# A linear-attention and gated-MLP mixer on one core: operands of the spatial products laid at equal residues, sums in place, a fixed order at the stage border

## The chip, the core and the metric

The kernel runs on one core of one Trainium2 chip. The core has five engines that run their own queues in order: TensorE (PE; its weight loads are listed as PEld), VectorE (DVE), ScalarE (ACT), GpSimd (POOL) and SyncE (SP, which here only issues transfers). They meet through semaphores. Data lie in SBUF (128 partitions) and PE writes to PSUM (8 banks of 512 floats per partition). A matmul has a stationary operand (at most 128 x 128, loaded first) and a moving one (128 x up to 512 columns). The metric is device time in microseconds (us) of one execution; the median of several runs is compared.

## The reference

All numbers are float32. After a layernorm of x, the outputs of two mixers are added to x:

```python
xn = _layernorm(x)                       # x: 1 x 2048 x 512
# A: linear attention, 32 heads of 16, phi = softmax(+) and softmax(-) of a per-head projection
num = einsum(phi_q, phi_k^T v);  den = einsum(phi_q, sum phi_k) + 1e-6;  A = (num / den) @ wo
# B: gated MLP with a spatial product over the 2048 tokens
z = gelu(xn @ w_in)                      # 2048 x 1376, halves z1 and z2 of 688 columns
z2 = layernorm(z2)
g = einsum("ts,bsf->btf", w_sp, z2) + b_sp[None, :, None]   # 2048 x 2048 times 2048 x 688
B = (z1 * g) @ w_out
return x + A + B
```

## The kernel before

Every product is computed from operands split into two parts, h (rounded to float32r) and l (what is left over). `mm3` (line 55) issues three matmuls for one product: h by h, h by l and l by h, lines 57, 58 and 59 in the profile. `round_h` (line 47) makes h, on ACT at line 49, and `rest_l` (line 52) makes l on DVE, line 53; `b_parts` (line 592) is the pair of them. The l part reads the h part, so DVE waits for ACT each time.

There are four stages. The first projects q, k, v and z1 and gathers the attention's sums. The second (loop at line 738) projects z2 from the weight tile w2 with `zproj` (line 138): 16 rows s of 128 tokens, each 2 halves of 344 columns (FC), tile zps in PSUM. ACT applies gelu and the normalisation (`normed`, line 730), and after every second s `b_split` (line 707) makes the moving operands of the spatial stage from the pair n = s // 2. The third is the spatial stage. The fourth projects the gated rows and the attention's output and adds them up.

**The spatial stage** computes w_sp @ z2 with the seven products of a Strassen-Winograd scheme on 2 x 2 blocks. NC = 32 steps n, each one (i, q) of `SEQ`: i counts 8 pairs of output rows of 128 tokens, q 4 chunks of the contracted tokens (for the last i in the order 1, 2, 3, 0). In a step, `products` (line 790) issues for each of the seven products P1, P2, P6, P5, P7, P3, P4, in this order (`FORM`), two chunks k of three matmuls: 42 matmuls of 344 columns, into seven PSUM banks of g that accumulate over the four steps of an i. The stationary operands (A11, A12, A22, S1 to S4) come from w_sp, the moving ones (B11, B21, B22, T1 to T4) from z2. P1 is A11 by B11, P2 A12 by B21, P6 S2 by T2, P5 S1 by T1, P7 S3 by T3, P3 S4 by B22, P4 A22 by T4.

`load_a` (line 597) loads the raw weights of a step (tiles wf) through SP's queue, in two transfers of 256 KB, into tiles f0 and f1 with two buffers each. `prep_a` (line 606) makes the A operands of a step: four sums on DVE (lines 621 to 625) into a tile S of its own, and four roundings and remainders. The tile that holds a pair of them has all h parts, then all l parts, each part [names][2][128] floats. Steps of even n take them from the right pool ws, those of odd n from the left pool hl1, which lies where w2 was. `b_tile` (line 694) hands out tiles of 1408 floats (SL) for B operands, seen as [a][b][352]: a is h or l, b one of two operands. B11 of the pairs 2q and 2q+1 share a tile; B22 and B21, T1 and T3, T2 and T4 have one for each pair. `b_split` takes three differences per pair into T (lines 710, 714, 719), on DVE. Line 739 gives `zproj` the halves in reversed order for odd s, so that the four quarters of z lie in the order 0, 1, 3, 2.

The loop at line 887 has, for a step n: at the second step of an i the load of z1 on POOL's queue (`load_z1`), `products`, at the fourth step `drain` (line 801: one copy on ACT, seven combinations of the PSUM banks on DVE into the tile c), then `load_a(n + 3)` and `prep_a(n + 2)`, then `gate` (line 816: gelu on ACT, the product with c on DVE) and its `turn`, which transposes on DVE and stores u in eight transfers on SP (lines 837 and 839; on POOL for i = 6). Three steps from the end the preparation of the fourth stage begins (`stage_w`, `first_gate`).

Otherwise the order of the instructions on each engine is that of a scheduler which works on the program's order and its own estimate of time; `tc.issue_after` pins single instructions. At the border of the second and third stage the last pairs of B and the first steps of A are made by DVE and ACT at once, while PE works on the last zps and the first g.

SBUF is laid out by pools stacked from the left (cst, xz, w1 ...) and from the right (pad, ws, zw, w2 ...). A tile's first byte follows from the sizes of all tiles ahead of it; the tiles named pad and gap hold nothing and only shift what comes after.

Of the kernel before, what the change touches and what calls it, by code (L numbers as in the profile page):

```python
# [18 lines left out]
P = 128  # L19
# [22 lines left out]
def mixer(ctx: ExitStack, tc: tile.TileContext, x, x_t, wv, wqkT, phi_bd, wo, w_in, wst, b_r, w_out, out):  # L42
# [50 lines left out]
    cst.tile([P, 8], F32, name="pad")  # L93
# [44 lines left out]
    def zproj(ps, s, w, order=(0, 1), wide=False):  # L138
# [15 lines left out]
        for k, j in enumerate(order):  # L154
            for c in range(ND):
                cs = slice(c * P, (c + 1) * P)
                zproj.last = mm3(p[k][:, :FC], (t[:, 0, cs], t[:, 1, cs]), (w[j][0][:, c], w[j][1][:, c]), c == 0, c == ND - 1)
# [386 lines left out]
    mid.enter_context(right("pad", 1)).tile([P, P + 8], F32, name="pad")  # L544
# [5 lines left out]
    w2_pool.tile([P, QP // 2], F32, name="gap")  # L550
# [41 lines left out]
    def b_parts(h, l, src):  # L592
        rounded = round_h(act, h, src)
        rest_l(l, src, h)
        return rounded

    def load_a(n):
        i, q = SEQ[n]
        f = []
        for k in range(2):  # L600
            t = ws.tile([P, QC, P], F32, tag=f"f{k}", bufs=2, name="wf")
            sp.dma_start(t, wst[2 * i + k, :, q * QC:(q + 1) * QC, :])
            f.append(t.rearrange("p (k two) t -> p two k t", two=2))
        return f

    def prep_a(n, f):
# [4 lines left out]

        def parts(names, src):
            t = pl.tile([P, 2, len(names), 2, P], F32R, tag="".join(names), name="A")
            prep_a.last = b_parts(t[:, 0], t[:, 1], src)
            for k, m in enumerate(names):
                ops[m] = t[:, 0, k], t[:, 1, k]

        sums = (sm[0].tile([P, 4, 2, P], F32, name="S") if sm else
                zw.tile([P, 4, FC], F32, tag=("T", "z2")[n], bufs=n + 1, name="S").rearrange("p a b -> p (a b)")[:, :8 * P].rearrange("p (a k b) -> p a k b", a=4, k=2))
        parts(("A11", "A12"), a)  # L620
        dve.tensor_tensor(sums[:, 0], b[:, 0], b[:, 1], op=ALU.add)
# [8 lines left out]
    hl, raw, A, sm = [ws, None], {}, {}, []  # L630
    NE = 2
    with ExitStack() as p1:
# [40 lines left out]
        A[0] = prep_a(0, raw.pop(0))  # L673
        sp.dma_start(kvT_d, kvT)
# [30 lines left out]
    B, b11 = [], None  # L705

    def b_split(z, n):
        nonlocal b11
        tt = zw.tile([P, 4, FC], F32, tag="T", name="T")
        dve.tensor_tensor(tt[:, 0:2], z[:, 1:3], z[:, 0:2], op=ALU.subtract)  # L710
        if n % 2 == 0:
            b11 = b_tile()
        b_parts(b11[:, 0, n % 2], b11[:, 1, n % 2], z[:, 0])
        dve.tensor_tensor(tt[:, 2], z[:, 2], tt[:, 0], op=ALU.subtract)
        ops = {"B11": (b11[:, 0, n % 2], b11[:, 1, n % 2])}
# [3 lines left out]
        dve.tensor_tensor(tt[:, 3], z[:, 3], tt[:, 2], op=ALU.subtract)  # L719
        t = b_tile()  # L720
        b_parts(t[:, 0], t[:, 1], tt[:, 0:2])
        ops["T1"], ops["T3"] = [(t[:, 0, k], t[:, 1, k]) for k in range(2)]
        t = b_tile()
        b_parts(t[:, 0], t[:, 1], tt[:, 2:4])
        ops["T2"], ops["T4"] = [(t[:, 0, k], t[:, 1, k]) for k in range(2)]
# [12 lines left out]
    for s in range(NT):  # L738
# [21 lines left out]
        if s == NT - 1:  # L760
            for k in range(2):
                normed(*late.pop(0), ins)
# [384 lines left out]
```

## Time and profile before

| what | value |
|---|---|
| runs of the kernel before | 612.50, 614.14, 614.09 us; median 614.09 |
| the profiled execution's own time | 613.86 us |
| its span (first to last instruction) | 612.1 us |
| granted TensorE clock | 1.000 |
| PE busy | 605.6 us (99%) |
| DVE busy | 520.0 us (85%) |
| ACT busy | 259.5 us (42%) |
| POOL busy | 132.4 us (22%) |
| spatial stage, first to last start of a matmul | 275.7 to 487.3 us |

Lines of a group read: source line, engine, operation, output <- inputs with shapes, count, then busy time, mean duration in ns and the engine's idle time ahead of them. For a tile they read: count, shortest/median/longest duration in ns, and the starts of the first and the last in us. Lines of the timeline read: start in us, duration in us, engine, line, operation, and in brackets how long the engine had been idle and what released it. A matmul's duration covers its way through the array, so consecutive ones overlap, and the pace of PE is the distance between starts. Lines with a window A:B give its length, then the busy time of each engine with its count of instructions, the clock, the share of the DMA engines and GB/s.

### The profile page before, as it was taken

How to read it: one execution, taken by the hardware profiler on the slowest of the kernel's cores; microseconds unless marked ns; L12 is line 12 of the kernel's file. 1: busy time of each engine (PE TensorE's matmuls, PEld its weight loads, DVE VectorE, ACT ScalarE, POOL GpSimd, SP SyncE). 2: the span in 40 equal slices, each digit the busy share in tenths (PEclk: the TensorE clock that was granted, in tenths of full speed). 3: DMA queues.
4: the chain of work that ended last, by engine and by line, in shares of the span. 5: the costliest groups of instructions: out<-in, count | busy, mean ns of one | idle time of the engine just before them, and what ended most of it. 6: DMA issues, size and time to landing. Idle time of an engine off the chain costs nothing.

```text
span 612.1 us, 11394 instructions
## 1 busy us (share of the span) xinstructions
PE 605.6 (99%) x4286; PEld 551.1 (90%) x4286; DVE 520.0 (85%) x930; ACT 259.5 (42%) x414; POOL 132.4 (22%) x231
## 2 busy tenths in 40 slices
PE   8999999999999999999999999999999999999997
PEld 6888888888888999999999999999999988777776
DVE  5999999999988578899888896877879999999932
ACT  4653324423433547887534433342335443332220
POOL 4122232333111014552000001000200041143430
PEclk9999999999999999999999999999999999999999
DMA  8557877566537848001455636555556899799792
GB/s 320 187 131 176 217 176 188 149 163 169 139 107 213 261 177 308 2 1 35 142 124 153 180 98 178 135 163 153 166 161 185 254 295 292 184 285 276 181 254 69
DMA packets 57950, 107.85 MB, mean 176 GB/s; under 512 B 12392, under 2 KB 24552, under 8 KB 57672
## 3 DMA queue, kind: packets, MB, share of 16 engines
q1 hardware_dynamic: 43656, 65.22, 35.3%
q0 software_dynamic: 11936, 36.28, 23.9%
q10 hardware_dynamic: 2304, 5.64, 2.4%
q8 instruction: 33, 0.54, 0.4%
q14 instruction: 21, 0.17, 0.1%
HBM read 66.85 MB, written 35.54 MB: 167 GB/s over the span
## 4 chain that ended last, share of the span: by engine, by line
PE 82%; DVE 8%; DMA 5%; issue 2%; ACT 1%; SPq 0%; POOL 0%; ACTq 0%; DVEq 0%; POOLq 0%
PE proj L58 7%; PE proj L57 7%; PE proj L59 7%; PE g L57 7%; PE g L58 7%; PE g L59 7%; PE zps L57 6%; PE zps L59 6%; PE zps L58 6%; PE pout L57 5%; PE pout L59 5%; PE pout L58 5%; DMA wf<-in_wst 3%; DVE A L53 2%; DMA z1t<-z_d 1%
## 5 line engine op out<-in xcount | busy, mean ns | idle before, releaser
L57 PE MATMUL g<-B,A 128*128 128x344 f32 x448 | 142.8, 320 | 0.6 <-DVE c L810 0.4
L58 PE MATMUL g<-B,A 128*128 128x344 f32 x448 | 142.3, 319 | 0.0
L59 PE MATMUL g<-B,A 128*128 128x344 f32 x448 | 138.9, 318 | 0.0
L57 PEld LDWEIGHTS g<-B,A 128*128 128x128 f32 x448 | 84.0, 188 | 1.6 <-DVE c L810 0.7
L58 PEld LDWEIGHTS g<-B,A 128*128 128x128 f32 x448 | 84.0, 188 | 0.0
L59 PEld LDWEIGHTS g<-B,A 128*128 128x128 f32 x448 | 83.6, 188 | 0.0
L49 ACT ACTIVATE A<-S 128x512 fp32r<-128x512 f32 x64 | 39.3, 628 | 74.8 <-DVE S L622 63.8
L57 PE MATMUL proj<-wqk_h,xT 128*128 128x512 f32 x128 | 50.1, 391 | 0.0
L59 PE MATMUL proj<-wqk_h,xT 128*128 128x512 f32 x128 | 49.8, 389 | 0.0
L58 PE MATMUL proj<-wqk_l,xT 128*128 128x512 f32 x128 | 49.8, 389 | 0.0
L125 ACT ACTIVATE e<-e,r_x 128x1024 f32<-128x1024 f32 x26 | 29.8, 1149 | 42.3 <-DVE e L124 41.3
L53 DVE TENSOR_TENSOR A<-S,A 128x512 fp32r<-128x512 f32 x64 | 42.8, 684 | 2.9 <-ACT A L49 2.8
L49 ACT ACTIVATE A<-wf 128x512 fp32r<-128x512 f32 (+1 forms) x64 | 32.7, 515 | 24.6 <-DMA wf<-in_wst 18.8
L57 PE MATMUL zps<-w1h,xT 128*128 128x344 f32 (+2 forms) x128 | 40.8, 320 | 0.0
L58 PE MATMUL zps<-w1l,xT 128*128 128x344 f32 (+2 forms) x128 | 40.7, 318 | 0.0
L59 PE MATMUL zps<-w1h,xT 128*128 128x344 f32 (+2 forms) x128 | 40.7, 318 | 0.0
L57 PE MATMUL zps<-w2h,xT 128*128 128x344 f32 (+2 forms) x128 | 40.7, 318 | 0.0
L58 PE MATMUL zps<-w2l,xT 128*128 128x344 f32 (+2 forms) x128 | 40.6, 317 | 0.0
L59 PE MATMUL zps<-w2h,xT 128*128 128x344 f32 (+2 forms) x128 | 40.3, 317 | 0.0
L53 DVE TENSOR_TENSOR A<-wf,A 128x512 fp32r<-128x512 f32 (+1 forms) x64 | 34.9, 550 | 4.9 <-ACT A L49 4.9
L128 DVE TENSOR_REDUCE sm<-e 128x64 f32<-128x1024 f32 x26 | 31.1, 1199 | 2.5 <-ACT e L125 2.5
L787 POOL DMA_DIRECT2D z1t<-z_d x16 | 9.1, 595 | 108.6 <-DMA wf<-in_wst 98.0
(219 smaller groups left out, 1432.2 us busy)
## 6 DMA issues: line engine op xcount, KB each, us to landing
wf<-in_wst SPq DMA_DIRECT2D x64, 256.0 KB, 3.5
e_d<-e POOLq DMA_DIRECT2D x16, 544.0 KB, 4.6
et<-e_d SPq DMA_DIRECT2D x16, 544.0 KB, 7.7
z_d<-z1f ACTq DMA_DIRECT2D x16, 344.0 KB, 3.4
z1t<-z_d POOLq DMA_DIRECT2D x16, 344.0 KB, 4.3
zacc<-e POOLq DMA_DIRECT2D x10, 512.0 KB, 4.8
u<-u_d SPq DMA_DIRECT2D x15, 320.0 KB, 5.4
xt<-in_x SPq DMA_DIRECT2D x16, 256.0 KB, 3.6
```

Of the source, the lines that this page charges most:

```text
L49: return act.activation(h, src, AF.Copy).ins
L53: return (eng or dve).tensor_tensor(l, src, h.bitcast(F32), op=ALU.subtract).ins
L57: pe.matmul(dst, ah, bh, start=start, stop=False)
L58: pe.matmul(dst, ah, bl, start=False, stop=False)
L59: return pe.matmul(dst, al, bh, start=False, stop=stop).ins
L125: softmax_pair.last = less, act.activation(e, e, AF.Exp, scale=scale).ins
L128: dve.tensor_reduce(sm, heads(e), axis=AX.X, op=ALU.add)
L787: pool.dma_start(t[:, k, :FH], z1_d[2 * i + k])
```

## The change

1. Residues. The operand tiles of A are allocated in another order (S4 and S3, A22, A11 and A12 with 32 floats (QP) more, S2 and S1), their layout becomes name by name with h and l of one name next to each other, and A11 is moved by 32 floats with q's parity. B11 of even and of odd pairs gets a tile of its own over two q's; `zproj` loses the reversed order, so that B21 comes first and B22 second in their tile. Pads change: 8 floats fewer in cst (all tiles of the left pools lie 32 bytes lower), 16 instead of 136 floats on the right, a gap of 48 instead of 16 floats behind w2, 32 floats ahead of hl1.
2. Sums in place. The four sums overwrite the raw weights, the tile S goes. Raw weights have three tiles in turn (f, x, y), and step n + 4 is loaded where n + 3 was.
3. Border. The differences of the last two pairs (n > 5) run on POOL, after the last rstd operation there. The normalisation of the last three rows is issued after step 0's products and the preparation of step 2. `in_turn` fixes the order on DVE and on ACT from step 1's sums to step 8's last operand, with the drain of i = 0 among them.
4. Drain. c22 is made from P7 and c12 instead of from P5 and c21, one place earlier; seven operations as before.
5. Last stage. The first output bank pout is allocated ahead of the others, the tiles of cw in another order; one pool tag has another name.

```diff
@@ cst, zproj, pads
-    cst.tile([P, 8], F32, name="pad")
-    def zproj(ps, s, w, order=(0, 1), wide=False):
+    def zproj(ps, s, w, wide=False):
-        for k, j in enumerate(order):
+        for k in range(2):
...
-    mid.enter_context(right("pad", 1)).tile([P, P + 8], F32, name="pad")
+    mid.enter_context(right("pad", 1)).tile([P, HP // 4], F32, name="pad")
-    w2_pool.tile([P, QP // 2], F32, name="gap")
+    w2_pool.tile([P, QP + HP // 4], F32, name="gap")
@@ load_a, prep_a
+    def spread(ap, axis, more):
+        dims = [list(d) for d in ap.ap]
+        dims[axis][0] += more
+        return bass.AP(ap.tensor, ap.offset, dims)
     def load_a(n):
         i, q = SEQ[n]
-        f = []
+        tag = "fx"[n] if n < 2 else "fxy"[(n - 2) % 3]
+        t = (fy[0] if tag == "y" else ws).tile([P, 2, QC, P], F32, tag="wf" + tag, name="wf")
         for k in range(2):
-            t = ws.tile([P, QC, P], F32, tag=f"f{k}", bufs=2, name="wf")
-            sp.dma_start(t, wst[2 * i + k, :, q * QC:(q + 1) * QC, :])
...
+            with tc.issue_after(load_a.last) if n == 5 else ExitStack():
+                load_a.last = sp.dma_start(t[:, k], wst[2 * i + k, :, q * QC:(q + 1) * QC, :]).ins
...
+        tiles = {}
+        for names, more in ((("S4", "S3"), 0), (("A22",), 0), (("A11", "A12"), QP), (("S2", "S1"), 0)):
+            tiles[names] = pl.tile([P, D * len(names) + more], F32R, tag="".join(names), name="A")
         def parts(names, src):
-            t = pl.tile([P, 2, len(names), 2, P], F32R, tag="".join(names), name="A")
-            prep_a.last = b_parts(t[:, 0], t[:, 1], src)
+            late = QP * (1 - SEQ[n][1] % 2) if "A11" in names else 0
+            more = QP if "A11" in names else 0
+            t = tiles[names][:, late:late + D * len(names)].rearrange("p (m l k t) -> p l m k t", l=2, k=2, t=P)
+            h, l = (spread(t[:, v], 1, more - late) for v in range(2))
+            prep_a.last = b_parts(h, l, src)
...
         parts(("A11", "A12"), a)
-        dve.tensor_tensor(sums[:, 0], b[:, 0], b[:, 1], op=ALU.add)
-        dve.tensor_tensor(sums[:, 1], sums[:, 0], a[:, 0], op=ALU.subtract)
-        parts(("S1", "S2"), sums[:, 0:2])
-        dve.tensor_tensor(sums[:, 2], a[:, 0], b[:, 0], op=ALU.subtract)
-        dve.tensor_tensor(sums[:, 3], a[:, 1], sums[:, 1], op=ALU.subtract)
-        parts(("S3", "S4"), sums[:, 2:4])
         parts(("A22",), b[:, 1:2])
+        a11, a12, a21, a22 = a[:, 0], a[:, 1], b[:, 0], b[:, 1]
+        turns[n, "first"] = dve.tensor_tensor(a22, a21, a22, op=ALU.add).ins,
+        dve.tensor_tensor(a21, a11, a21, op=ALU.subtract)
+        dve.tensor_tensor(a11, a22, a11, op=ALU.subtract)
+        turns[n, "sums"] = dve.tensor_tensor(a12, a12, a11, op=ALU.subtract).ins,
+        parts(("S2", "S1"), pair(a11, a22))
+        parts(("S4", "S3"), pair(a12, a21))
@@ order of the border
+    def in_turn(*keys):
+        for e in range(2):
+            queue = [turns[k][e] for k in keys if e < len(turns[k])]
+            for a, b in zip(queue, queue[1:]):
+                tc.add_manual_dep(b, a.name, mybir.DependencyInfo(
+                    mybir.DependencyClass.NoSync, mybir.DependencyReason.DATA), reason="order of the border")
@@ b_split
-        dve.tensor_tensor(tt[:, 0:2], z[:, 1:3], z[:, 0:2], op=ALU.subtract)
-        if n % 2 == 0:
-            b11 = b_tile()
+        eng = pool if n > 5 else dve
+        with tc.issue_after(b_split.after) if eng is pool else ExitStack():
+            eng.tensor_tensor(tt[:, 0:2], z[:, 1:4:2], z[:, 0:2], op=ALU.subtract)
+        k, q = n % 2, n // 2 % 2
+        if not q:
+            b11[k] = b_tile()
+        b = b11[k][:, 0, q], b11[k][:, 1, q]
...
-        ops["B22"], ops["B21"] = [(t[:, 0, k], t[:, 1, k]) for k in range(2)]
+        ops["B21"], ops["B22"] = [(t[:, 0, k], t[:, 1, k]) for k in range(2)]
...
@@ end of the second stage
-        if s == NT - 1:
-            for k in range(2):
-                normed(*late.pop(0), ins)
...
+    hl[1].tile([P, QP], F32, name="pad")
     A[1] = prep_a(1, raw.pop(1))
-    raw[2] = load_a(2)
-    normed(*late.pop(), ins)
-    ctx_zw.__exit__(None, None, None)
+    raw[3] = load_a(3)
...
+    products(0, g)
+    A[2] = prep_a(2, raw.pop(2))
+    while late:
+        normed(*late.pop(0), ins)
+    ctx_zw.__exit__(None, None, None)
+    gt = mid.enter_context(right("gt", 1))
+    fy.append(mid.enter_context(right("fy", 1)))
@@ loop of the spatial stage
-        if n + 3 < NC:
-            raw[n + 3] = load_a(n + 3)
-        if n + 2 < NC:
+        if n + 4 < NC:
+            raw[n + 4] = load_a(n + 4)
+        if 0 < n < NC - 2:
             A[n + 2] = prep_a(n + 2, raw.pop(n + 2))
+        if n == 6:
+            in_turn((1, "sums"),
+                    ("B", 6, 2),
+                    (2, "A11"),
+                    (1, "S2"), (1, "S4"),
+                    ("B", 7, 1),
+                    (2, "A22"), (2, "first"), (2, "sums"), (2, "S2"), (2, "S4"),
+                    ("B", 6, 3), ("B", 6, 4),
+                    ("B", 7, 2),
+                    (3, "A11"), (3, "A22"), (3, "first"), (3, "sums"), (3, "S2"), (3, "S4"),
+                    ("B", 7, 3), ("B", 7, 4),
...
@@ last stage
+    pso = ctx.enter_context(psum("pso", 1))
+    pout = [pso.tile([P, D], F32, tag="out", bufs=2, name="pout")]
     pst = ctx.enter_context(psum("pst", 4))
-    pso = ctx.enter_context(psum("pso", 1))
...
-            p = pso.tile([P, D], F32, tag="out", bufs=2, name="pout")
+            p = pout.pop() if pout else pso.tile([P, D], F32, tag="out", bufs=2, name="pout")
```

More of the change, by code (lines that the diff above doesn't have):

```diff
@@ L593, in b_parts @@
         rounded = round_h(act, h, src)
[L594 removed]
+        b_parts.pair = rest_l(l, src, h), rounded
         return rounded
+    def spread(ap, axis, more):
+        dims = [list(d) for d in ap.ap]
+        dims[axis][0] += more
+        return bass.AP(ap.tensor, ap.offset, dims)
     def load_a(n):
         i, q = SEQ[n]
[L599 removed]
+        tag = "fx"[n] if n < 2 else "fxy"[(n - 2) % 3]
+        t = (fy[0] if tag == "y" else ws).tile([P, 2, QC, P], F32, tag="wf" + tag, name="wf")
         for k in range(2):
[L601 to L604 removed]
+            with tc.issue_after(load_a.last) if n == 5 else ExitStack():
+                load_a.last = sp.dma_start(t[:, k], wst[2 * i + k, :, q * QC:(q + 1) * QC, :]).ins
+        return [t[:, k].rearrange("p (k two) t -> p two k t", two=2) for k in range(2)]
     def prep_a(n, f):
@@ L615, in parts, with pair @@
             for k, m in enumerate(names):
-                ops[m] = t[:, 0, k], t[:, 1, k]
-        sums = (sm[0].tile([P, 4, 2, P], F32, name="S") if sm else
-                zw.tile([P, 4, FC], F32, tag=("T", "z2")[n], bufs=n + 1, name="S").rearrange("p a b -> p (a b)")[:, :8 * P].rearrange("p (a k b) -> p a k b", a=4, k=2))
+                ops[m] = h[:, k], l[:, k]
+        def pair(x, y):
+            (first, kd, td), more = x.ap, y.offset - x.offset
+            return bass.AP(x.tensor, x.offset, [first, [more, 2], kd, td])
@@ new lines, in prep_a @@
+        a11, a12, a21, a22 = a[:, 0], a[:, 1], b[:, 0], b[:, 1]
[5 more added lines that the diff above has]
+        parts(("S4", "S3"), pair(a12, a21))
+        return ops
+    hl, raw, A, fy, turns = [ws, None], {}, {}, [], {}
@@ L673, in mixer @@
         A[0] = prep_a(0, raw.pop(0))
+        raw[2] = load_a(2)
         sp.dma_start(kvT_d, kvT)
@@ L724, in b_split @@
         b_parts(t[:, 0], t[:, 1], tt[:, 2:4])
+        turns["B", n, 4] = b_parts.pair
         ops["T2"], ops["T4"] = [(t[:, 0, k], t[:, 1, k]) for k in range(2)]
@@ L738, in mixer @@
     for s in range(NT):
-        p = zproj((kv_ps_p, zc, zbp, za)[s % 4], s, w2, (0, 1) if s % 2 == 0 else (1, 0), s == 0)
+        p = zproj((kv_ps_p, zc, zbp, za)[s % 4], s, w2, wide=s == 0)
         if s < NT - 2:
@@ L806, in drain @@
         first = act.activation(c12, g["P1"], AF.Copy)
-        add(c11, g["P2"], b1, c12)
-        dve.tensor_tensor(c21, g["P6"], c12, op=ALU.add)
-        dve.tensor_tensor(c12, g["P5"], c21, op=ALU.add)
-        dve.tensor_tensor(c21, g["P7"], c21, op=ALU.add)
-        add(c22, g["P5"], b2, c21)
-        add(c12, g["P3"], b1, c12)
+        steps = [add(c11, g["P2"], b1, c12),
+                 dve.tensor_tensor(c21, g["P6"], c12, op=ALU.add),
+                 dve.tensor_tensor(c12, g["P5"], c21, op=ALU.add),
+                 add(c22, g["P7"], b2, c12),
+                 dve.tensor_tensor(c21, g["P7"], c21, op=ALU.add),
+                 add(c12, g["P3"], b1, c12)]
         drained = add(c21, g["P4"], b2, c21)
+        for k, x in enumerate(steps + [drained]):
+            turns["c", i, k] = x.ins,
         return cb, first.ins, drained.ins
@@ L890, in mixer @@
             z = load_z1(i)
-        products(n, g)
+        if n:
+            products(n, g)
         if n % NQ == NQ - 1 and i < NP - 1:
@@ L940, in fetch_u, with f_pair @@
                       cw.tile([2 * REM, P], F32R, tag="rt", bufs=6, name="rt"))
-    def er_pair(name):
-        return cw.tile([P, 2, NF], F32, tag="er", bufs=3, name=name)
+    def f_pair():
+        return cw.tile([P, 2, NF], F32, tag="f", bufs=3, name="f")
     def features(s):
```

39 lines of the change are left out of this document (20 added, 19 removed), and 13 rows, old and new, of the table g.

## The prediction

> **What bounds the kernel now.** I read the page first, for the engine that never rests.
>
> ```profile
> span 612.1 us, 11394 instructions
> PE 605.6 (99%) x4286; PEld 551.1 (90%) x4286; DVE 520.0 (85%) x930; ACT 259.5 (42%) x414; POOL 132.4 (22%) x231
> PEclk9999999999999999999999999999999999999999
> L57 PE MATMUL zps<-w1h,xT 128*128 128x344 f32 (+2 forms) x128 | 40.8, 320 | 0.0
> ```
>
> TensorE (PE) is busy for 605.6 of 612.1 us at the full granted clock in every slice. A change can win in two ways only: by the few us in which PE stands still, or by matmuls that follow each other faster. The mean of 320 ns in a row is no pace, since matmuls overlap; the pace is the distance between starts. So the second view is the spatial stage alone, the matmuls that write g, first whole and then from 336 to 452 us.
>
> ```profile
> L57 PE MATMUL g<-B,A x448: 314/318/427, 275.7 to 487.0; 128*128 128x344 f32 x150
> L57 PE MATMUL g<-B,A x249: 314/318/324, 335.7 to 452.0; 128*128 128x344 f32 x125
> ```
>
> Every third matmul is of this line, 448 of 1344. In the window, 248 distances of three matmuls take 116.3 us: 469.0 ns for three, 156.3 ns for one. At that pace the 447 of the whole stage would take 209.6 us; from 275.7 to 487.0 they take 211.3, so 1.7 us are standstill.
>
> The third view is the timeline of PE for another group of the same shape, 344 columns: the projection zps, at two places. Nine matmuls lie between the two rows of each fence.
>
> ```profile
> 237.84 0.32 PE L59 MATMUL zps<-w2h,xT 128*128 128x344 f32 x1
> ...
> 239.22 0.32 PE L59 MATMUL zps<-w2h,xT 128*128 128x344 f32 x1
> ```
>
> ```profile
> 208.25 0.32 PE L59 MATMUL zps<-w1h,xT 128*128 128x344 f32 x1
> ...
> 209.67 0.32 PE L59 MATMUL zps<-w1h,xT 128*128 128x344 f32 x1
> ```
>
> Nine in 1.38 us is 153.3 ns each; nine in 1.42 us is 157.8. One shape, one clock, two paces. In these projections every offset is a multiple of 512 bytes, so the moving and the stationary operand keep one relation throughout. In the spatial stage they don't. A tile of B is 1408 floats and its second operand starts 352 floats in: 1408 bytes, five and a half times 256. All operands of A lie at multiples of 512 bytes. So half of the products have operands that agree modulo 256 bytes (by the layout both pools start at byte 192 of 256), and half lie 128 bytes apart. Step 9 starts at 335.26 us and shows both kinds:
>
> ```profile
> 335.57 0.31 PE L59 MATMUL g<-B,A 128*128 128x344 f32 x1
> 335.72 0.32 PE L57 MATMUL g<-B,A 128*128 128x344 f32 x1
> ...
> 337.14 0.32 PE L57 MATMUL g<-B,A 128*128 128x344 f32 x1
> ...
> 338.98 0.32 PE L57 MATMUL g<-B,A 128*128 128x344 f32 x1
> ```
>
> The nine from 335.72 (B11 with its second half, and P2) are 128 bytes apart: 1.42 us, 157.8 ns each. The twelve from 337.14 (P6 and P5) agree: 1.84 us, 153.3 each. That speaks for the change. Step 8 speaks against a simple rule: the same twelve agreeing matmuls of P6 and P5 start at 330.54 and end their run at 332.43.
>
> ```profile
> 330.54 0.32 PE L57 MATMUL g<-B,A 128*128 128x344 f32 x1
> ...
> 332.43 0.32 PE L57 MATMUL g<-B,A 128*128 128x344 f32 x1
> ```
>
> 1.89 us, 157.5 each. So agreement allows the fast pace, but what ran before decides whether it is taken. Once taken it lasts while the relation does: all of zps around 238 us keeps it.
>
> **The change part by part.** *Agreement.* Afterwards every product's operands agree: the tile for A11 and A12 has 32 floats more and shifts by them with q's parity, the tile for S2 and S1 lies 128 bytes off the others, B21 and B22 trade places. Two residues remain (160 and 32 of 256), and the pair switches from one to the other and back once per step, twice in 42 matmuls. Taken at the fast pace: 1344 x (156.3 - 153.3) = 4.0 us saved. The ends are 0 (nothing gained) and, if all go slow, 1344 x 1.5 = 2.0 us lost. I take the fast end, nearest to the twelve of step 9 and to zps; a switch is not in this trace; between nothing and three matmuls at the slow pace, 3 x 4.5 ns, the 64 of them cost 0 to 0.9 us.
>
> *Standstill.* The largest is in step 28:
>
> ```profile
> 461.65 0.32 PE L59 MATMUL g<-B,A 128*128 128x344 f32 x1
> ...
> 463.44 0.32 PE L58 MATMUL g<-B,A 128*128 128x344 f32 x1
> ...
> 464.07 0.32 PE L59 MATMUL g<-B,A 128*128 128x344 f32 x1
> 464.82 0.42 PE L57 MATMUL g<-B,A 128*128 128x344 f32 x1 [0.43 <-DVE c L810]
> 465.08 0.31 PE L58 MATMUL g<-B,A 128*128 128x344 f32 x1
> ```
>
> From 461.65 to 465.08 lie 14 distances: 3.43 us against 14 x 0.1563 = 2.19, so 1.2 us lost in three waits for A. The queue of SP and VectorE (DVE) say why A was late:
>
> ```profile
> 447.13 2.09 SPq L837 DMA_DIRECT2D u_d<-z1t  x4
> 450.10 2.70 SPq L839 DMA_DIRECT2D ur_d<-z1t  x4
> 452.89 10.16 SPq L602 DMA_DIRECT2D wf<-in_wst  x6
> ```
>
> ```profile
> 456.57 0.42 DVE L621 TENSOR_TENSOR S<-wf 128x256 f32<-128x256 f32 x1 [3.22 <-DMA wf<-in_wst]
> ```
>
> The loads of the spatial weights stand behind eight transposed stores on SP, and DVE then idles 3.22 us for one. The change loads step n+4 where it loaded n+3: one step, 42 x 0.153 = 6.4 us, earlier, more than 3.22. The third raw tile pays for it: load n+4 takes the tile of n+1, as load n+3 does today with two. I take the 1.2 us as gone; what is late next is the drain of g on DVE (the 0.43 above), at worst 0.4 of it stays. Of the other 0.5 us, at the border, 0.3 goes with the fixed order.
>
> *Border on GpSimd (POOL).* Six differences leave DVE. Their cost there:
>
> ```profile
> 277.34 0.88 DVE L710 TENSOR_TENSOR T<-z 128x688 f32<-128x688 f32 x1
> 279.14 0.51 DVE L714 TENSOR_TENSOR T<-z,T 128x344 f32<-128x344 f32 x1
> ```
>
> A large one and two small ones per pair, 0.88 + 2 x 0.51 = 1.9 us: 3.8 us off DVE, all beside PE's work. On POOL no such operation is in the trace. The nearest:
>
> ```profile
> L187 POOL TENSOR_TENSOR mask<-mask 128x128 f32<-128x128 f32 x1 | 0.5, 457 | 0.1
> 273.82 0.27 POOL L758 TENSOR_SCALAR nb<-mv,rstd 128x1 f32<-128x1 f32 x1
> 279.76 1.16 POOL L758 TENSOR_SCALAR nb<-mv,rstd 128x1 f32<-128x1 f32 x1
> ```
>
> An estimate from these: at best as on DVE, 1.9 us per pair; at worst 457/128 = 3.6 ns an element, 1376 elements, 4.9 per pair. Both pairs take 3.8 to 9.8 us, and start when the last nb ends, 279.76 + 1.16 = 280.9. The operation on one element took 0.27 us once and 1.16 beside a busy DVE; if each of the six lost 0.9 so, 5.4 more. They end between 284.7 and 296.1, then 0.9 each on ACT and DVE. P6 of step 3 needs the last at 275.7 + (126 + 12) x 0.1533 = 296.9. So even the worst sum is late by only 1.0 us; I take 0. The fixed order adds a wait: DVE stands at T of pairs 6 and 7 for POOL, and behind it in its queue stand A of steps 3 and 4, for which PE would wait. The Trainium skill, SBUF — State Buffer, section Who interferes with whom, speaks against this move: a DVE instruction with two SBUF inputs contends with a GpSimd instruction that reads SBUF. The 0.27 and 1.16 us agree with it.
>
> *In place.* Same four sums, same roundings; a sum may overwrite only after ACT's rounding, but DVE's remainder ahead of it waits for that already. Cost 0, covered by DVE's slack:
>
> ```profile
> 322.10:348.40 26.30, 22.69 (x47) 1.00 0.55 150
> ```
>
> Four steps (here 26.30 us with 22.69 of DVE) would take 168 x 0.1533 = 25.8 us: DVE stays under PE. The drain keeps its seven operations: 0. *Last stage.* PE is busy 32.00 of 32 us there, so the new layout has nothing to hide:
>
> ```profile
> 488.00:520.00 32.00, 32.00 (x212) 25.66 (x211) 30.58 (x48) 11.75 (x22) 7.94 (x13) 1.00 0.95 288
> ```
>
> DVE is nearest to the bound there with 30.58, unchanged by the edit. Every left tile moves by 32 bytes; moving and stationary operands of the projections move together, 0.
>
> **Sum.** The profiled execution took 613.86 us, 1.8 more than its span and 0.2 under the median of 614.09. 613.86 - 4.0 - 1.2 - 0.3 = 608.4 us. With the dear switch (0.9) and 0.4 of step 28 it is 609.7; should the new start bytes shorten the fast pace to some 151 ns, about what a single distance in step 9 shows (335.57 to 335.72), 1344 x 2.3 ns = 3.1 less, 605.3.
>
> **The rivals.** *The relation is not the cause.* The two paces would come from something else, and g keeps 156.3 on average. For it: step 8's slow agreeing run. Against: step 9, and zps. Only the standstill goes: 612.4 us. The Trainium skill, TensorE: Matmul & The Clock Gate, section Step-by-step: what each phase is for, has such a rule: the two operands come through two independent read ports, so that loading the next weights takes no bandwidth from the running matmul. The trace disagrees, with 153.3 and 157.8 ns.
>
> *The slow pace takes hold.* Each switch of residue, or the new residues themselves, leave PE at 157.8. For it: after the wait the agreeing matmuls from 463.44 to 464.07 run four in 0.63 us, 157.5; and 208 us is slow for long. In g alone: 612.4 + 2.0 = 614.4 us, no change; half fast and half slow, 611.4. If zps takes it too, having moved by the same 32 bytes, its six rows of 128 add 768 x 4.5 ns = 3.5: 617.9 us, slower. This ends on the other side once more than about 7.3 of the 9.5 us between the two paces are lost. Against: where the relation stays, zps returns to the fast pace and keeps it.
>
> *POOL holds the border.* If its operations cost twice the worst estimate, 19.6 us, the last ends at 300.5, is ready at 302.3, and PE waits 5.4 us in step 3: 613.8 us. Against: that is 7 ns an element.
>
> **How the numbers follow.** Forecast 0.58; relation not the cause 0.14; slow pace 0.20, of it 0.10 in g alone and 0.10 in zps too; POOL 0.08. About 0.3% (1.8 us) is what a measurement tells from no change, so faster means under 612.0 and slower over 615.7. Faster: 0.58, half of the slow pace in g (0.05), most of POOL (0.06): 0.69. Slower: zps and g slow, 0.10, and 0.03 for a border wait on top of the slow pace. Same: 0.18. The range reaches from 605.0 to 614.4: it takes in all but the slow zps.
>
> **What would show it.** Right: g's rows 206 to 207 us from first to last start; three matmuls in 460 ns in every step, both parities alike; no distance over 0.2 us in step 28; DVE's idle for wf there under 3.22; zps still 153.3; POOL's differences ended before 296. Wrong: g at 156 or more with long agreeing runs at 157.8; PE waiting in steps 3 or 4 with DVE waiting for POOL; zps slow.

## The result and the profile after

| what | before | after |
|---|---|---|
| median of the runs | 614.09 us | 619.61 us (616.98, 620.85, 621.49, 619.61, 619.45) |
| ratio after : before | | 1.0106, interval 1.0088 to 1.0123: slower, by 1.1% |
| the profiled execution's own time, its span | 613.86, 612.1 us | 616.98, 615.3 us |
| spatial stage, first to last start of a matmul | 275.7 to 487.3 us | 275.5 to 490.1 us |
| mean distance of its matmuls without the waits | 156.4 ns | 154.2 ns |
| what the waits add to that | 1.5 us | 7.5 us |

The profiled execution is the fastest of the five; the other four had spans of 617.7 to 619.8 us and a mean granted clock of 0.996 to 0.999 instead of 1.000 (experiment e13 shows one source of such a loss). So the trace explains the 3.1 us between the two profiled executions; of the 5.5 us between the medians, 2.4 stand in no trace. The page of after begins:

```profile
span 615.3 us, 11377 instructions
PE 604.2 (98%) x4286; PEld 548.7 (89%) x4286; DVE 527.9 (86%) x924; ACT 260.4 (42%) x414; POOL 140.8 (23%) x237
```

PE works 1.4 us less than before and the span is 3.2 us longer: the gain is there, and more than it is lost in waiting. By parts, from the starts of all matmuls: pace 1344 x (154.2 - 156.4) = -3.0 us, waits +5.9, the end after the last matmul +0.4 (4.17 instead of 3.74), all else -0.3; before rounding +3.1 together, as the profiled times have it. The tile g in the window of the prediction (count, shortest/median/longest ns, first and last start), and two rows of step 28 from the timeline of PE:

```profile
L59 PE MATMUL g<-B,A x254: 313/316/348, 334.7 to 451.7; 128*128 128x344 f32 x127
```

```profile
464.60 0.32 PE L58 MATMUL g<-B,A 128*128 128x344 f32 x1
...
465.98 0.32 PE L58 MATMUL g<-B,A 128*128 128x344 f32 x1
```

253 distances of three take 117.0 us, 154.2 ns for one. In step 28 nine take 1.38 us, 153.3 each, and no wait stands there. So where are the waits? The view of what PE waited for, from 275 to 325 us, names the start of the stage:

```profile
PE g L57 <- ACT A L49: 2.0, 3, 1.0
PE g L59 <- DVE A L53: 1.3, 1, 1.3
PE g L57 <- DVE c L836: 1.2, 1, 1.2
PE g L57 <- ACT B L49: 0.6, 1, 0.6
```

They lie in steps 1, 3, 4 and 6. Two chains lead there. First POOL and the instructions on DVE beside it:

```profile
280.58 1.91 POOL L734 TENSOR_TENSOR T<-z 128x688 f32<-128x688 f32 x1
282.57 1.44 POOL L741 TENSOR_TENSOR T<-z,T 128x344 f32<-128x344 f32 x1
284.09 1.24 POOL L747 TENSOR_TENSOR T<-z,T 128x344 f32<-128x344 f32 x1
292.26 2.25 POOL L734 TENSOR_TENSOR T<-z 128x688 f32<-128x688 f32 x1 [6.94 <-DVE B L53]
294.60 1.26 POOL L741 TENSOR_TENSOR T<-z,T 128x344 f32<-128x344 f32 x1
295.93 0.99 POOL L747 TENSOR_TENSOR T<-z,T 128x344 f32<-128x344 f32 x1
```

```profile
280.87 2.36 DVE L53 TENSOR_TENSOR B<-z,B 128x688 fp32r<-128x688 f32 x1
283.15 3.33 DVE L53 TENSOR_TENSOR A<-wf,A 128x512 fp32r<-128x512 f32 x3
...
292.89 3.25 DVE L53 TENSOR_TENSOR A<-wf,A 128x512 fp32r<-128x512 f32 x2
296.17 1.04 DVE L637 TENSOR_TENSOR wf<-wf 128x256 f32<-128x256 f32 x1
...
300.30 1.66 DVE L53 TENSOR_TENSOR B<-T,B 128x688 fp32r<-128x688 f32 x2
306.13 1.03 DVE L53 TENSOR_TENSOR A<-wf,A 128x512 fp32r<-128x512 f32 x2 [4.17 <-ACT A L49]
```

A pair's differences take 4.6 and 4.5 us on POOL, inside the estimate of 1.9 to 4.9. But the second pair waited 6.94 us for its tile: T exists once, and DVE read the first pair's T until 292. And wherever POOL worked, DVE was late: 2.36 us for a remainder of 688 columns, 1.04 for a sum that otherwise takes 0.42.

The two engines take turns, a whole instruction each; neither just runs slower. Two remainders on DVE, each by itself:

```profile
292.89 2.18 DVE L53 TENSOR_TENSOR A<-wf,A 128x512 fp32r<-128x512 f32 x1
294.99 1.15 DVE L53 TENSOR_TENSOR A<-wf,A 128x256 fp32r<-128x256 f32 x1
```

POOL's three differences of this pair end at 294.51, 295.86 and 296.92. The two remainders and the sum at 296.17, which ran beside them, end 0.55, 0.28 and 0.29 us after that. The other way round, POOL's second and third difference end 0.79 us after the DVE instruction that was under way when they began, and its first 1.5 us after. All six traces with differences on POOL (after, e2, e4, e6, e11, e12) repeat this: where the two overlap, POOL ends 1.51 to 1.55 us after DVE's instruction for 688 columns and 0.77 to 0.80 for 344, and DVE ends 0.73 us after POOL's for 688 columns, 0.55 for 512 and 0.28 to 0.29 for 256. So a difference on POOL adds its own time to DVE's queue. An estimate from these figures: 1.5 + 2 x 0.8 = 3.1 us for a pair, 6.2 for both.

The second chain is the hole of 4.17 us at 306.13. DVE waited for ACT, and ACT for step 4's weights:

```profile
305.47 1.07 ACT L49 ACTIVATE A<-wf 128x512 fp32r<-128x512 f32 x2 [2.97 <-DMA wf<-in_wst]
```

Step 4 is the first to use the third raw tile (y). The reading with which the experiments below began was that y lies where T lay, so that its load could not start before the last T had been read, at about 302 us. The addresses of the compiled program say otherwise: y takes bytes 190752 to 194848 of a partition, T 200800 to 206304. In y's place lay z of pair 6, which POOL's third difference of that pair is the last to read, until 285.33 us. What holds the load is its place in SP's queue, whose order there is step 6, step 4, step 5. Step 6's load takes the tile of step 3 and waits for the last remainder made from it, on DVE until 300.32. The first transfer for step 6, then the first for step 4:

```profile
300.35 0.33 SPq L607 DMA_DIRECT2D wf<-in_wst  x1
301.35 0.38 SPq L607 DMA_DIRECT2D wf<-in_wst  x1
```

### The profile page after: what moved, and what is told of

It reads as the page before. It is cut to its first block, busy times and chain, and to the rows that moved or that the text cites. A ratio compares the mean times of both kernels' runs of the same rounds, so it can differ in the third digit from the quotient of the medians.

```text
span 615.3 us, 11377 instructions
## 1 busy us (share of the span) xinstructions
PE 604.2 (98%) x4286; PEld 548.7 (89%) x4286; DVE 527.9 (86%) x924; ACT 260.4 (42%) x414; POOL 140.8 (23%) x237
## 4 chain that ended last, share of the span: by engine, by line
PE 79%; DVE 7%; issue 4%; ACT 3%; POOL 3%; DMA 3%; SPq 0%; POOLq 0%; ACTq 0%; DVEq 0%
PE g L57 9%; PE g L59 9%; PE g L58 9%; PE proj L57 7%; PE proj L58 7%; PE proj L59 7%; PE pout L57 5%; PE pout L59 5%; PE pout L58 5%; PE zps L59 2%; PE zps L58 2%; PE zps L57 2%; DVE A L53 2%; PE po L1062 1%; PE pout L1083 1%
## 5 line engine op out<-in xcount | busy, mean ns | idle before, releaser
L57 PE MATMUL g<-B,A 128*128 128x344 f32 x448 | 141.1, 318 | 3.8 <-ACT A L49 2.0
L58 PE MATMUL g<-B,A 128*128 128x344 f32 x448 | 141.2, 317 | 0.0
L59 PE MATMUL g<-B,A 128*128 128x344 f32 x448 | 136.1, 318 | 1.5 <-DVE A L53 1.3
L49 ACT ACTIVATE A<-wf 128x512 fp32r<-128x512 f32 (+1 forms) x128 | 70.0, 573 | 114.2 <-DVE wf L639 66.3
L53 DVE TENSOR_TENSOR A<-wf,A 128x512 fp32r<-128x512 f32 (+1 forms) x128 | 80.1, 648 | 13.4 <-ACT A L49 12.9
L124 ACT ACTIVATE e<-e,r_x 128x1024 f32<-128x1024 f32 x26 | 29.7, 1148 | 41.8 <-DVE e L123 40.8
L57 PE MATMUL pout<-wu,uh 128*128 128x512 f32 x75 | 30.4, 406 | 0.0
L59 PE MATMUL pout<-wu,ul 128*128 128x512 f32 x75 | 29.3, 390 | 0.0
```

What stands on the lines that cost most here:

```text
L49: return act.activation(h, src, AF.Copy).ins
L53: return (eng or dve).tensor_tensor(l, src, h.bitcast(F32), op=ALU.subtract).ins
L57: pe.matmul(dst, ah, bh, start=start, stop=False)
L58: pe.matmul(dst, ah, bl, start=False, stop=False)
L59: return pe.matmul(dst, al, bh, start=False, stop=stop).ins
L124: softmax_pair.last = less, act.activation(e, e, AF.Exp, scale=scale).ins
```

## The experiments

**The theories.** After the first reading of the profile, theory 1 put all new waits down to POOL; its rival blamed the order written out by hand. The step behind the hole at 306 us, the load of step 4, came out of the first runs.

**e1_dve_diff: the change, but all differences on DVE.**

```diff
-        eng = pool if n > 5 else dve
+        eng = dve
```

> The changed kernel with the six differences of the last two pairs of B back on VectorE; all else as changed. Theory 1 (GpSimd's differences hold the border, by slowing VectorE's operations beside them and by making the last tile T late): the standstill of PE in steps 1 to 6, 7.5 us in the changed kernel's profile, falls under 1.5 us, VectorE's roundings there go back to 0.7 to 0.9 us, and the time is 607 to 610 us. Rival 2 (the fixed order itself is the cause): at least 4 of the 7.5 us stay, 613 us or more. Rival 3 (sums in place, or the load of step 4 in room that is freed late): the wait in step 1 goes, those in steps 3 and 4 stay, some 612 to 615 us.

Measured: 616.39 us, ratio 1.0050 (1.0032 to 1.0068). The waits of steps 1 and 3 are gone, that of step 4 is not: 4.8 us, where the whole change has 3.1. The timeline of DVE:

```profile
283.81 0.87 DVE L53 TENSOR_TENSOR B<-z,B 128x688 fp32r<-128x688 f32 x1
284.60 1.89 DVE L53 TENSOR_TENSOR A<-wf,A 128x512 fp32r<-128x512 f32 x3
...
293.68 1.03 DVE L53 TENSOR_TENSOR A<-wf,A 128x512 fp32r<-128x512 f32 x2
...
295.04 0.43 DVE L637 TENSOR_TENSOR wf<-wf 128x256 f32<-128x256 f32 x1
...
304.85 1.17 DVE L53 TENSOR_TENSOR A<-wf,A 128x512 fp32r<-128x512 f32 x2 [4.34 <-ACT A L49]
```

The same four groups without POOL: 0.87, 1.89, 1.03 and 0.43 instead of 2.36, 3.33, 3.25 and 1.04 us. So beside POOL DVE lost 5.8 us, close to the estimate of 6.2 and more than the 3.8 us of differences it was rid of. That part of theory 1 holds; that POOL was the whole cause does not, since the hole of 4.34 us stands there without POOL.

**e2_free_order, e3_dve_free: without the order by hand; e3 with the differences on DVE too.**

```diff
-        if n == 6:
-            in_turn((1, "sums"),
...
```

> The changed kernel without the fixed order; GpSimd keeps the differences. Theory 1: GpSimd still slows VectorE and the second trio of differences still waits for the tile T, so at least 4 us of standstill stay in steps 1 to 6, 613 us or more. Rival 2 (the order is the cause): under 1.5 us of standstill, 607 to 610 us.

> Differences on VectorE and no fixed order: the border as the scheduler lays it, with equal residues and sums in place. Theory 1: 607 to 611 us, with up to 2 us of standstill at the border, since nothing now puts the early operands first. Rival 3 (sums in place, late room for step 4's load): 612 us or more with PE waiting in steps 3 and 4.

Measured: e2 613.15 us, 1.0005 (0.9996 to 1.0015), waits of 4.3 us in steps 1 and 2; e3 612.01 us, 0.9984 (0.9969 to 1.0000), 1.4 us of waits, in step 2. Neither shows a wait in step 4. e3's time is 1 us above the range of theory 1, and its wait lies in neither of the steps that the rival named. In both, SP's order is step 4, 5, 6. In e3 the first transfer for step 4 leaves 10 us earlier than in e1 (299.75), into the same tile y; behind it DVE's last remainder made from T:

```profile
289.45 0.43 SPq L607 DMA_DIRECT2D wf<-in_wst  x1
```

```profile
293.45 0.87 DVE L53 TENSOR_TENSOR B<-T,B 128x688 fp32r<-128x688 f32 x1
```

It has landed at 293.10, before DVE's last reading of T has begun. So T does not hold y's room, and without the fixed order there is no late load. By which rule the scheduler put step 6's load first is not shown.

**e4_before_pool: the kernel before, with only the last two pairs' differences on POOL.**

```diff
+        eng = pool if n > 5 else dve
+        with tc.issue_after(b_split.after) if eng is pool else ExitStack():
-        dve.tensor_tensor(tt[:, 0:2], z[:, 1:3], z[:, 0:2], op=ALU.subtract)
+            eng.tensor_tensor(tt[:, 0:2], z[:, 1:3], z[:, 0:2], op=ALU.subtract)
```

> The kernel before with one part of the change alone: the six differences on GpSimd, after its last rstd operation. Theory 1: the two-input operations of VectorE beside them take up to 2 us each instead of 0.4 to 0.9, PE waits 3 to 8 us in steps 1 to 4, 617 to 622 us. Rivals 2 and 3: no fixed order and a separate tile for the sums here, so within 1.5 us of 614.1 us.

Measured: 618.38 us, 1.0081 (1.0062 to 1.0101); 7.5 us of waits and slow distances, the new ones in steps 1 and 2. The move to POOL costs time in the kernel before too, without any other part of the change.

**e5_room, e6_room_pool, e7_room_free: step 4's weights in tile f**, which is free after step 2's operands are made; the third tile is first used by step 6. e5 is e1 with it, e6 the whole change with it, e7 is e3 with it.

```diff
-        tag = "fx"[n] if n < 2 else "fxy"[(n - 2) % 3]
+        tag = "fxfxfx"[n] if n < 6 else "yfx"[(n - 6) % 3]
...
-        if n + 4 < NC:
+        if n + 4 < NC and n != 1:
             raw[n + 4] = load_a(n + 4)
         if 0 < n < NC - 2:
             A[n + 2] = prep_a(n + 2, raw.pop(n + 2))
+        if n == 1:
+            raw[5] = load_a(5)
```

> Differences on VectorE, fixed order kept, and the raw weights of step 4 go to the tile of step 2 instead of the third one, whose room the last tile T of the second stage holds; step 5's load follows step 3's preparation. Theory 1b (besides GpSimd, the load of step 4 waits for the last read of T, which the fixed order puts late): PE's standstill in steps 3 and 4, 5.1 us in the run with the differences on VectorE, falls under 1.5 us, and the time to 609 to 611.5 us. Rival (the fixed order is late by itself, whatever the room): 3 us or more of it stay, 614 us or more.

> The changed kernel, GpSimd and fixed order kept, with step 4's weights in the tile of step 2 alone. Theory 1b: the waits of step 1 and of step 3's P6, which GpSimd causes, stay (4 us or more), those at the start of step 4 go: 613 to 616 us, against 616.98 to 621.49 of the changed kernel. Rival (room alone is the cause): 611 us or less.

> Differences on VectorE, no fixed order, step 4's weights in the tile of step 2. With the scheduler's order the last T is read earlier already, so theory 1b expects little of the room here: 610.5 to 612 us, as without it (612.0), standstill at the border 0.5 to 2 us.

Measured: e5 610.61 us, 0.9958 (0.9943 to 0.9972), faster than the kernel before; e6 614.00, 1.0019 (1.0005 to 1.0034); e7 613.02, 0.9992 (0.9982 to 1.0003). e7 misses its expectation of 612 at most. The timeline of DVE in e5 has no hole; step 4's operands and sums follow at once:

```profile
300.28 1.02 DVE L53 TENSOR_TENSOR A<-wf,A 128x512 fp32r<-128x512 f32 x2
301.33 0.43 DVE L637 TENSOR_TENSOR wf<-wf 128x256 f32<-128x256 f32 x1
```

e5 and e6 came out as theory 1b had it, but not for its reason, since T never held the room. With tile f for step 4, SP's order is step 4, 5, 6, and e5's first transfer for step 4 leaves at 290.49, behind the last remainder of step 2's operands. Of the kernels with three raw tiles, only after and e1 have ahead of step 4's load one that waits for step 3.

By the medians the two causes add up: the late load 616.39 - 610.61 = 5.8 us (e1 and e5), POOL 614.00 - 610.61 = 3.4 us (e6 and e5), and 610.61 + 5.8 + 3.4 = 619.8 against 619.61 measured for the whole change. The traces show less of each, and an overlap. All waits together are 6.3 us in e1, 5.4 in e6 and 2.6 in e5, so 3.6 and 2.7 more; in the whole change they are 7.5 and not 8.9, because PE has waited 3.6 us in steps 1 and 3 already when it comes to step 4. Why e7 is not better than e5 stays open: both profiles have 2.6 us of waits and the profiled runs took 612.0 and 612.3 us, but the medians are 2.4 us apart.

**e8_apart: e3 with every pair of spatial operands 128 bytes apart.** The pads move the raw weights, z and T by 128 bytes too; the projections' operands keep their relation.

```diff
-    mid.enter_context(right("pad", 1)).tile([P, HP // 4], F32, name="pad")
+    mid.enter_context(right("pad", 1)).tile([P, QP + HP // 4], F32, name="pad")
...
-    w2_pool.tile([P, QP + HP // 4], F32, name="gap")
+    w2_pool.tile([P, HP // 4], F32, name="gap")
...
-    hl[1].tile([P, QP], F32, name="pad")
```

> Differences on VectorE, no fixed order, but pads moved so that all operands of the spatial products lie 128 bytes apart (160 against 32 and 32 against 160); the projections keep theirs. Theory (agreement sets the pace): the mean distance of the spatial matmuls, waits aside, goes from 154.2 to 157 to 158 ns and the time from 612.0 to 616 to 617.5 us. Rival (the pace comes from something else): 154.2 ns and 612 us stay.

Measured: 615.24 us, 1.0038 (1.0025 to 1.0051), against 0.9984 for e3; somewhat less than forecast. The tile g of e3, then of e8:

```profile
L59 PE MATMUL g<-B,A x254: 313/316/321, 334.8 to 451.7; 128*128 128x344 f32 x127
```

```profile
L59 PE MATMUL g<-B,A x249: 314/318/325, 334.8 to 451.7; 128*128 128x344 f32 x125
```

In the same 116.9 us e3 makes 253 distances of three and e8 248: 154.0 and 157.1 ns for one. The rival by which the relation is not the cause is out.

**e9_lead3: e5 with weights loaded three steps ahead, as before, from step 9 on.**

```diff
-        if n + 4 < NC and n != 1:
-            raw[n + 4] = load_a(n + 4)
+        if n < 8 and n != 1:
+            raw[n + 4] = load_a(n + 4)
+        if n > 8 and n + 3 < NC:
+            raw[n + 3] = load_a(n + 3)
```

> e5_room, but from step 9 on the weights are loaded three steps ahead (n + 3) as before the change, instead of four. The prediction's own step: the load one step earlier is what removes the standstill of step 28 (1.2 us). By it the waits of step 28 come back: distances over 0.2 us there, 1.2 us together, span 609.0 to 610.6 + 1.2. Rival: the third raw tile alone frees the load and the lead makes no difference, because SP issues the load at the same place behind the eight stores: no distance over 0.2 us in step 28, and the same time as e5_room within 0.5 us.

Measured: 610.72 us, 0.9962 (0.9948 to 0.9975), and no wait in step 28. So the load one step earlier is not needed to remove that wait.

**e10_tail: e5 with the last stage's tiles and first output bank ordered as before.**

```diff
     f_pair()
-    cw.tile([P, KF * P], F32, tag="u", bufs=4, name="u")
+    wo_h = cw.tile([P, ND, D], F32R, name="woh")
+    cw.tile([2 * REM, P], F32R, tag="rt", bufs=6, name="rt")
...
-    pout = [pso.tile([P, D], F32, tag="out", bufs=2, name="pout")]
```

> e5_room with the last stage's tiles and its first output bank ordered as before the change (part 5 undone). All kernels with the changed last stage end 4.17 us after the last matmul's start, the kernel before 3.74. If part 5 is the reason, the tail is 3.74 again and the time 0.4 us less than e5_room. If it is the 32 bytes by which all left tiles lie lower, the tail stays 4.17 and the time is the same. Either way the stretch from 490 us to the last matmul stays 121.0 us within 0.2.

Measured: 613.42 us, 0.9997 (0.9978 to 1.0016). Both theories missed: the end stays 4.17 us, and the stretch from 483.8 us, the last g, to the last matmul grows from 120.9 to 122.6. The timelines of PE and of ACT:

```profile
493.42 0.50 PE L57 MATMUL pout<-woh,oT 128*128 128x512 f32 x1 [0.32 <-ACT oT L49]
```

```profile
492.25 0.63 ACT L49 ACTIVATE woh<-wof 128x512 fp32r<-128x512 f32 x1 [2.34 <-DMA wof<-in_wo]
492.79 1.07 ACT L49 ACTIVATE oT<-po 128x512 fp32r<-128x512 f32 x2
```

ACT waits 2.34 us for a weight in its queue, oT stands behind it, and PE waits for oT. That may be the old order of the tiles, but it isn't shown: e13, which has the new one, takes 122.6 us there as well, with waits for oT on DVE. The 2.8 us between the medians are more than the 1.7 us that the profile shows.

**e11_pair7, e12_pair6: e5 with one pair's differences on POOL**, the last, and the one before.

```diff
-        eng = dve
+        eng = pool if n == 7 else dve
```

> e5_room with only the last pair's three differences on GpSimd (n == 7). Theory (each pair's differences on GpSimd delay what DVE does beside them, and the fixed order passes that on): step 1 shows no wait, and step 3 shows waits for P2 and P6 of up to 2.9 us as with both pairs there: 611 to 614 us. Rival (only the first pair matters, because the second trio is late only through the first one and the one T tile): no distance over 0.2 us in steps 1 to 3 and 610.6 us.

> e5_room with only the first of the last two pairs' differences on GpSimd (n == 6). Theory (each pair has its own price): step 1 waits for P6 2.2 to 2.5 us as with both pairs on GpSimd, and step 3 shows no wait: 612.5 to 613.5 us. Rival (the price belongs to the second trio and T): step 1 waits less than 0.5 us, 610.6 us.

Measured: e11 612.24 us, 0.9979 (0.9965 to 0.9994), PE waiting in step 3; e12 612.08 us, 0.9983 (0.9969 to 0.9997), PE waiting in step 1, none in step 3. Each pair makes PE wait in its own step, as the theory had it. By the medians each costs about half of the 3.4 us, hardly more than the intervals allow; e12's time and its wait of 1.4 us are below what the expectation gave. DVE in e11, then in e12:

```profile
292.15 3.25 DVE L53 TENSOR_TENSOR A<-wf,A 128x512 fp32r<-128x512 f32 x2
295.43 1.04 DVE L637 TENSOR_TENSOR wf<-wf 128x256 f32<-128x256 f32 x1
```

```profile
280.69 2.35 DVE L53 TENSOR_TENSOR B<-z,B 128x688 fp32r<-128x688 f32 x1
282.96 3.35 DVE L53 TENSOR_TENSOR A<-wf,A 128x512 fp32r<-128x512 f32 x3
```

The long instructions come singly: each trio on POOL holds up its own neighbours, by the same amount as in the whole change.

**e13_two_tiles: e5 with two raw tiles, sums still in place.**

```diff
-        tag = "fxfxfx"[n] if n < 6 else "yfx"[(n - 6) % 3]
+        tag = "fx"[n % 2]
...
+        if n > 2 and n + 3 < NC:
+            raw[n + 3] = load_a(n + 3)
```

> e5_room with two raw tiles in turn instead of three (from step 6 on the weights of step n + 3 take the tile of step n + 1, as before the change), sums still in place. If the third tile removed the standstill of step 28, distances over 0.2 us come back in the steps in which the weights stand behind the stores, step 28 above all, 1 us or more together, and the time is 611.7 or more. If the sums in place or the new order of the instructions did, step 28 shows none and the time is that of e5_room, 610.6, within 0.5 us. In both cases the mean distance stays 154.0 to 154.2 ns.

Measured: 624.02 us, 1.0163 (1.0132 to 1.0195); 14.8 us of waits and slow distances from step 4 to step 31, only 0.7 of them in step 28. With two tiles the sums in place cost more than all else here. But the scheduler also put the instructions in another order, so the price is that of the whole kernel, and not of the tile alone. The end after the last matmul is 3.76 us here. After distances of 2.3 us in step 15 and 1.0 and 1.3 in step 16, the timeline of PE shows another thing:

```profile
388.32 0.49 PE L57 MATMUL g<-B,A 128*128 128x344 f32 x1
388.61 0.49 PE L58 MATMUL g<-B,A 128*128 128x344 f32 x1
...
391.19 0.49 PE L58 MATMUL g<-B,A 128*128 128x344 f32 x1
```

Ten distances in 2.87 us: 287 ns each, almost twice the usual; an eleventh follows, then the pace returns. e4 has ten such distances too, after 3.5 us of waits at the end of step 1 and the start of step 2. Both executions had a mean clock of 0.997, and four of the five of after had 0.996 to 0.999. That the same happened there is argued, since they left no trace, and it doesn't explain their times: the slowest, 621.49 us, had 0.999, and in e1 three executions with 0.994 to 0.996 took 615.4 to 617.0 us, the profiled one with 1.000 took 616.62. The Trainium skill, TensorE: Matmul & The Clock Gate, section Part 1: The HAM clock gate, has PE's clock at half while the array was little busy of late; 287 against 154 ns agrees.

**e14_before_low: the kernel before with all left tiles 32 bytes lower.**

```diff
-    cst.tile([P, 8], F32, name="pad")
```

> The kernel before without its first pad of 8 floats, so that all left tiles lie 32 bytes lower and nothing else changes. If that shift makes the end longer, the tail after the last matmul's start is 4.17 us instead of 3.74, and the time 0.4 us more; if not, it is 3.74. The spatial operands then agree in no product (they lie 32 or 96 bytes off an agreement, instead of 0 and 128): if agreement to the byte is what allows the fast pace, the mean distance of g rises from 156.4 to about 157.8 ns, 1.9 us more; if only the larger distance of 128 bytes is slow, it falls or stays. zps stays 153.3 ns where it was, its two operands both being on the left.

Measured: 614.20 us, 1.0017 (1.0005 to 1.0030). The end stays 3.73 us, so the shift is not what lengthens it. My layout was wrong in one point: B lies on the left as well, so that in odd steps, whose A lies there too, half of the products still agree; in even steps none does. From the starts, an even step takes 6.606 us without a wait (157.3 ns) and an odd one 6.554 (156.0), against 6.587 and 6.540 before. Fewer agreeing products, a slower step; 32 bytes apart are no better than 128. The expectation was wrong on zps as well: its weight w2 lies on the right and xT on the left, so they come to lie 32 bytes apart, and from 235 us on the distance is 156.7 ns where it was 153.3. The tile zps from 235 us on, in before, then in e14:

```profile
L59 PE MATMUL zps<-w2h,xT x89: 316/316/316, 235.1 to 275.6; 128*128 128x344 f32 x89
```

```profile
L59 PE MATMUL zps<-w2h,xT x90: 317/318/318, 234.8 to 276.6; 128*128 128x344 f32 x90
```

88 distances of three take 40.5 us before, 89 take 41.8 in e14. Step 28 shows no wait in this kernel. But DVE idles 2.93 us for the weights there as well; PE only comes to step 28 later, at 461.38 us instead of 459.94.

## Why the prediction was wrong

Forecast were 608.4 us, in a range of 605.0 to 614.4; 619.61 were measured, against 614.09 before. The gain in pace came, and more than that was lost in waits at the border.

**The pace** was right in direction and three quarters of the size: 156.4 to 154.2 ns, 3.0 us where I took 4.0. The full fast pace is there in single steps: step 24 takes 6.442 us, 153.4 ns. But a switch of residue costs one distance of 157 to 158 ns, and in some steps the matmuls after it stay slower (step 27: 155.7 ns). These are the dear switches: I gave them 0 to 0.9 us, took 0, and they cost about 1.1. About 0.3 of it is the one distance at each of the 64 switches, by the 4.5 ns between the two paces; the rest are slow stretches behind some of them, such as the one from the middle of step 26 to the middle of step 27. Of the rivals, that by which the relation is not the cause is out (e8, and zps in e14). The slow pace does take hold, but only until a later switch; zps keeps 153.3 ns in after.

**Step 28** lost its 1.2 us, but not for my reason: with three raw tiles, loads three steps ahead do as well (e9). What removes the wait is not settled. The traces show that the eight stores ahead of the loads begin 1.8 us before step 26 in e9 and 0.3 us after its start in the kernel before, where DVE had waited 2.66 us for the gate's gelu of z1. e14 says nothing here, since its load is late too and PE later.

**The border** is where the prediction failed, in two of its terms: POOL's differences, and the early load. It wrote of POOL: "So even the worst sum is late by only 1.0 us; I take 0." The durations on POOL were inside the estimate; two other things were missing from the sum. I let the second pair follow the first without a gap, though T exists once and DVE had to have read the first pair's: 6.94 us of waiting. And I priced POOL's side of the contention alone. I had read the rows 0.27 and 1.16 us as POOL held up by DVE; e1 and after show DVE held up by POOL, 0.87 and 2.36 us for the same remainder. The Trainium skill, SBUF — State Buffer, section Who interferes with whom, does not say that it is always POOL that has to wait: "Issue order, not op shape, decides who blocks." The trace agrees: the two take turns, and DVE waited for POOL's work, 5.8 us in all. So the move cost DVE more than the 3.8 us that it took off. The rival that POOL holds the border had the right engine and too small a chance, 0.08, and asked for twice the worst duration on POOL, which was not needed. It is worth 3.4 us (e5 and e6).

**The early load** I put at one step earlier everywhere and paid for by the third raw tile, because "load n+4 takes the tile of n+1". That holds in the steady state. At the border the load of step 4 was late instead: it stood in SP's queue behind that of step 6, which waits for step 3's operands, and left at 301.35 us into a tile that was free since 285.33. None of my rivals had this; at 5.8 us by the medians (e1 and e5), 4.2 by the waits of step 4 in their traces (4.8 and 0.6), it is the larger of the two causes. My sentence on the fixed order, that PE would wait for A of steps 3 and 4 behind DVE, named the right steps with the wrong releaser. With step 4's load in time the order does no harm: e5, with it, has the lowest median of all, and e9 is level with it.

**In place** was forecast to cost nothing. No kernel here has it alone, so that isn't shown; DVE's slack shrank. A window of after, with the busy time of PE, PEld and DVE behind its length:

```profile
322.00:348.40 26.40, 25.80 (x167) 25.53 (x167) 24.62 (x54) 11.58 (x21) 1.07 (x2) 1.00 0.55 151
```

DVE is busy 24.62 of 26.40 us where it was 22.69 of 26.30, but seven more of its instructions fall in the window (54, not 47). Over the whole execution, e5 has DVE busy for 525.1 us against 520.0 before, with 930 instructions in both. **The last stage** takes 121.0 us as before. The 0.4 us more behind it I had not foreseen. It stands in every kernel here with three raw tiles (4.11 to 4.18 us) and in none with two (3.73 to 3.76: before, e4, e13, e14); neither the shift (e14) nor the order of the tiles (e10) makes it, and by which path the third tile does stays open.

**What is left of the change.** With the differences on DVE and step 4's weights in tile f, the change gains 2.6 us (e5: 610.61 against 613.24 us, 0.9958) and comes within 2.2 us of the forecast; its trace still has 2.6 us of waits, in steps 4, 6 and 15.

## What to carry to other kernels

When work is moved to an idle engine, price also what it does to the instructions that run beside it, and look for the one buffer that the moved work shares with its readers. When loads are moved, read the order in which they stand in their queue, at the start of a stage above all: one that waits holds up those behind it, and the steady state tells nothing about it. A fix that works isn't yet the cause: e5 removed the wait by way of the queue's order, and the room that it was meant to gain had been free all along. An order fixed by hand is only as good as the durations and releases it was written for: with it one late load became a wait of PE, and it was harmless once the load was early.

## What the runs showed of the hardware

- A switch of the operands' residue modulo 256 bytes costs one distance of 157 to 158 ns among those of 153 to 154; where the two operands differ by 32 or 128 bytes the mean is 156.7 to 157.3 ns (e8 and e14).
- POOL's subtractions of two SBUF operands and DVE's instructions with two take turns. DVE's ends 0.73, 0.55 or 0.28 us after POOL's, for 688, 512 or 256 columns, and so takes 2.36 us instead of 0.87, 2.18 instead of 0.69, or 1.04 instead of 0.43; POOL's ends 1.5 us after DVE's for 688 columns, 0.8 for 344.
- After PE had waited for 3.5 us within 5 us (e4) and for some 4.2 us within 11 us (e13), its distances were 287 ns for ten and eleven matmuls; in e1's profile 4.2 us of waits within 7 us were not followed by it, so the bound is not known.
- The four sums in place start 0.46 us apart on DVE, also where one only overwrites what the one before has read; before, two sums that share no output start 0.34 apart. The timeline of DVE in after, then in before:

```profile
327.29 0.42 DVE L638 TENSOR_TENSOR wf<-wf 128x256 f32<-128x256 f32 x1
327.75 0.42 DVE L639 TENSOR_TENSOR wf<-wf 128x256 f32<-128x256 f32 x1
```

```profile
324.24 0.42 DVE L621 TENSOR_TENSOR S<-wf 128x256 f32<-128x256 f32 x1
324.58 0.42 DVE L624 TENSOR_TENSOR S<-wf 128x256 f32<-128x256 f32 x1
```
